# Nyström attention with two expert layers on one core: the same steps in a new hand-written order

## The chip, the cores and the metric

The kernel runs on one core of a Trainium2 chip. The metric is the time of one execution in device microseconds (us). The core's engines are TensorE (PE, with its weight loads shown apart as PEld), VectorE (DVE), ScalarE (ACT), GpSimd (POOL) and SyncE (SP); each works through an instruction queue of its own in order, and they wait for one another by semaphores. Transfers between the chip's memory (HBM) and the on-chip memory (SBUF) run on 16 DMA engines and are issued by SP (stores at the end also by ACT). Products of PE land in PSUM.

## The reference

```python
def _attn_ref(q, k, v):                      # [4, 8, 576, 64], m = 32 landmarks
    q_lm = q.reshape(B, H, m, S // m, D).mean(axis=3)
    k_lm = k.reshape(B, H, m, S // m, D).mean(axis=3)
    A, Bm, C = sm(q, k_lm), sm(q_lm, k_lm), sm(q_lm, k)      # softmaxes
    Z = Bm.transpose(0, 1, 3, 2) / (norm1(Bm) * norminf(Bm) + 1e-06)
    for _ in range(6):
        Z = 2 * Z - Z @ Bm @ Z
    return A @ Z @ C @ v

def _moe_ref(x, w_in, w_out):                # 2304 tokens, 512 -> 2048 -> 512
    h = x @ w_in
    return (h * np.tanh(softplus(h))) @ w_out

def _moe2_ref(x, w_in, w_out):
    g = np.maximum(x @ w_in, 0.0) ** 2
    return g @ w_out
```

The output of the attention, with its heads side by side, is the input x of the first layer, and the first layer's output that of the second.

## The kernel before

The kernel is one straight program without loops on the chip. Its order is written out by hand: the string `PROGRAM` holds 2638 steps of the form `thing.step@tag+n`, and the last lines of the function call them one after the other under a manual schedule, so that each engine's queue holds its instructions in the order in which the steps issue them. `@tag` names the PSUM buffer of the step's result; `+n` puts n products of the identity with itself into that buffer ahead of the step (line 311, warm-ups). Buffers are taken from lists of free ones by tag, so a transfer's issue on SP waits until the work on the buffer's former tile is done, and the entries behind it on SP wait too.

Eight head groups, `a` to `h`, of four heads each go through the attention: `lk`, `lq`, `lv` load (L491 to L525), `tk`, `tq` turn k and q by products with the identity (L569), `tl` makes the landmark means, `pa`, `pb`, `pc` are the scores (L716, L642, L657), `pe` turns the exponentials (L682; `ET` copies them out of PSUM on ACT), `pv` multiplies them with v (L697). The groups form three batches `B0`, `B1`, `B2`; the last, the third head group of the title's change, holds four of them, `e` to `h` (their tiles end in 20, 21, 30, 31: pe31 and pv31 are those of `h`). A batch runs the six Newton steps: `n` is the product (L848, tiles nw20 to nw25 of B2), `r` copies one half of it on ACT (L861), `z` adds the other half on DVE (L865), and the next `n` needs both; `pw` (L883) and `wz` then put Z into the weights, and the folds `F` (L912) multiply these into layer 1's w_in. So each Newton step is short work on PE followed by a way over ACT and DVE, and other steps stand between two of them to keep PE at work.

Layer 1 works on pieces of tokens: `p.f` makes the hidden products (`hc`), `t.y` the products with w_out (`y`), both with three fp32r products for one fp32 product (`prod`, L930 to L932); `U` units load a weight block of 512 KB (`d`, L364 or L375), split it into a high and a low part on ACT, DVE and POOL (`lo`, `st`, `ab`, `cl`, `ad`, `hi`, `lw`). Layer 2 runs over combined halves of its matrices (a scheme with seven products for eight blocks): `W`, `X`, `Y`, `Q` and `Z` are its parts; `Q..a` and `Q..b` load weights that the kernel itself stored in HBM (L1272, L1298), `Q..p` are products with w_in (L1283 to L1285), `Q..d` sums of them on DVE (L1313), `Q..y` products with w_out into tiles O20, O21, O22 (L1356 to L1358), `Z.e` the last sums on DVE (L1250), `Z.o` the stores of the output (L1257).

Of the kernel before, what the change touches and what calls it, by code (L numbers as in the profile page):

```python
# [10 lines left out]
F32 = mybir.dt.float32  # L11
F32R = mybir.dt.float32r
U32 = mybir.dt.uint32
# [41 lines left out]
    U3.lo c.zk@y B0.n0@at B0.r0 B0.z0 U4.cl B0.n1@y+3 b.mi b.ae B0.r1 U3.st U3.ab c.xq c.zq c.TL B0.z1 B0.n2@at B0.r2
    U4.ad e.lk b.su U3.cl U3.ad d.lk B0.z2 b.pe@h b.mu B0.n3@y+2 d.sk U4.hi U4.lw c.pc@h b.ET b.lv c.pb@at c.PB b.pv@y
    B0.r3 B0.z3 B0.n4@y B0.r4 b.tb c.pa@at+1 b.ah B0.z4 B0.n5@y U0.ad d.tk@h c.cm B0.z5 b.cv d.Sk B0.pw@y U8.d U8.lo
    c.at e.lq d.Tk B0.wz d.tl@y d.TL c.ce c.am c.mi e.tk@h+1 e.Tk e.sq d.pc@at d.cm b.al d.pb@y d.PB B1.bx U5.d U5.lo
    c.pe@h U5.st f.lk U6.d@gh c.ET B1.be F00.fo@h c.ae d.ce B1.bs B1.nr@y+7 U8.st B1.rs d.pe@at f.lq B1.n0@y F00.mh
    f.tk@h U5.ab d.lv U5.cl e.Sq U5.ad U7.ab U8.ab d.ET B1.z0 B1.r0 F00.ml B1.n1@y d.pa@at B1.z1 U6.lo U6.st B1.r1  # L60
    B1.n2@y f.Tk U6.ab U7.cl U7.ad p0.f0 U5.hi c.cr B1.z2 d.at c.lv p0.f1 p0.f2 B1.r2 U6.cl p0.M0 B1.n3@y B1.r3 d.cr
    d.am U6.ad U6.hi e.lv U6.lw p0.f3 p0.M1 f.sq e.tq@h U7.hi U7.lw e.Tq B1.z3 d.pv@y d.cv f.tq@at c.pv@y e.sk p0.c0
    p0.g0 f.Tq B1.n4@y B1.r4 p1.f0 e.Sk p0.c1 B1.z4 c.su p1.f1 p1.M0 p1.c0 p1.f2 B1.n5@at B1.z5 U5.lw p1.g0 e.tl@y
    p0.g1 e.TL p1.f3 c.cv B1.pw@y B1.wz e.pc@h U8.cl U8.ad d.mi p1.M1 p1.c1 p1.g1 e.pb@at e.PB f.sk e.cm c.mu U9.d
# [1394 lines left out]
```

## Time and profile before

| | before |
|---|---|
| median of the runs | 785.86 us (785.80 to 786.46) |
| profiled execution | 784.31 us |
| its span, first to last instruction | 782.2 us |
| PE busy | 763.4 us, 5952 matmuls |
| DVE busy | 613.6 us |
| POOL, ACT busy | 387.0 us, 376.1 us |
| DMA moved | 156.73 MB, mean 200 GB/s |
| mean granted clock of PE | 0.994 |

PE is busy for 98% of the span; the 18.8 us without PE work and the stretches at a lower granted clock are what an order of the same steps can change. A fp32 product of plain operands shows as two matmuls in the trace (a Newton step of 16 products as 32), a fp32r product as one. Times in the timeline are starts and lengths from the span's start; "issue" as a releaser means that the engine waited for nothing that the profile shows. Matmul lengths overlap in the pipeline, so the text takes differences of starts.

### The profile page before, as it was taken

Reading aid. Unit: us, or ns where it says so; the run is one execution under the profiler, and the core shown is the slowest. Engines: PE = TensorE matmul, PEld = TensorE weight load, DVE = VectorE, ACT = ScalarE, POOL = GpSimd, SP = SyncE. Lnnn points to the kernel's source line nnn. Section 1 sums busy time; section 2 is a strip of 40 time slices with the busy share of each in tenths; the row PEclk is TensorE's granted clock in tenths of the full one; section 3 lists DMA queues with packets and bytes.
Section 4 is the critical chain, followed back from the end, with each engine's and each line's share of the span. In section 5 each row is a group of like instructions: output and inputs, shape, how many; then the busy total and the mean of one; then the engine's idle time right before and its main releaser. Section 6 shows DMA issues by size and latency. Waiting matters only on the chain.

```text
span 782.2 us, 15515 instructions
## 1 busy us (share of the span) xinstructions
PE 763.4 (98%) x5952; PEld 713.0 (91%) x5952; DVE 613.6 (78%) x964; ACT 376.1 (48%) x622; POOL 387.0 (49%) x265
## 2 busy tenths in 40 slices
PE   6999999899999999999999999999999999999997
PEld 5778989698999999999999988999999999999996
DVE  7899877488686877779789889866786888776785
ACT  6798887454674564646553333342333331332240
POOL 2544332242333543525466877786464585635440
PEclk9999999899999999999999999999999999999999
DMA  9672462201231455666729898898988797668853
GB/s 323 214 223 85 132 187 82 83 28 55 82 108 54 149 188 176 228 203 230 243 94 300 246 297 251 282 307 293 301 268 277 224 307 250 225 223 271 276 171 81
DMA packets 87721, 156.73 MB, mean 200 GB/s; under 512 B 9184, under 2 KB 37088, under 8 KB 87648
## 3 DMA queue, kind: packets, MB, share of 16 engines
q1 hardware_dynamic: 86976, 154.96, 61.1%
q10 hardware_dynamic: 672, 0.79, 0.4%
q8 instruction: 47, 0.77, 0.4%
q14 instruction: 26, 0.21, 0.1%
HBM read 119.54 MB, written 36.18 MB: 199 GB/s over the span
## 4 chain that ended last, share of the span: by engine, by line
PE 93%; DMA 3%; DVE 2%; ACT 1%; issue 1%; SPq 0%; POOL 0%; ACTq 0%; DVEq 0%; POOLq 0%
PE y L930 9%; PE y L931 8%; PE y L932 8%; PE P L1283 7%; PE P L1285 7%; PE P L1284 7%; PE hc L930 5%; PE hc L931 4%; PE hc L932 4%; PE O L932 4%; PE O L931 4%; PE O L930 4%; PE O L1358 3%; PE O L1357 3%; PE O L1356 3%; PE m L912 2%
## 5 line engine op out<-in xcount | busy, mean ns | idle before, releaser
L1177 POOL TENSOR_TENSOR ringglx<-A,ringghx 128x768 fp32r<-128x768 f32 x40 | 76.7, 1936 | 63.9 <-ACT ringghx L1172 63.9
L1172 ACT CAST ringghx<-A 128x768 fp32r<-128x768 f32 x40 | 33.0, 836 | 78.8 <-DVE A L1149 27.5
L1313 DVE TENSOR_TENSOR U<-U,P 128x384 f32<-128x384 f32 x72 | 39.8, 552 | 36.4 <-PE P L1285 35.0
L932 PE MATMUL O<-b,ringglx 128*128 128x256 f32 x240 | 67.8, 282 | 0.0
L931 PE MATMUL O<-b,ringghx 128*128 128x256 f32 x240 | 67.8, 282 | 0.0
L981 DVE TENSOR_TENSOR ringglx<-sc,ringghx 128x576 fp32r<-128x576 f32 (+2 forms) x80 | 63.5, 820 | 5.3 <-ACT ringghx L976 5.3
L930 PE MATMUL O<-b,ringghx 128*128 128x256 f32 x240 | 67.7, 282 | 0.0
L1015 DVE TENSOR_TENSOR acc<-acc,y 128x384 f32<-128x384 f32 x72 | 39.3, 549 | 30.9 <-PE y L932 30.7
L963 ACT ACTIVATE sc<-hc 128x576 f32<-128x576 f32 x64 | 41.4, 654 | 40.6 <-PE hc L932 28.0
L976 ACT CAST ringghx<-sc 128x576 fp32r<-128x576 f32 (+2 forms) x80 | 44.1, 576 | 18.2 <-PE y L932 17.4
L932 PEld LDWEIGHTS O<-b,ringglx 128*128 128x128 f32 x240 | 45.8, 191 | 0.0
L931 PEld LDWEIGHTS O<-b,ringghx 128*128 128x128 f32 x240 | 45.7, 191 | 0.0
L930 PEld LDWEIGHTS O<-b,ringghx 128*128 128x128 f32 x240 | 45.7, 190 | 0.0
L1313 DVE TENSOR_TENSOR A<-U,P 128x384 f32<-128x384 f32 x56 | 30.1, 549 | 19.3 <-PE P L1285 15.9
L410 POOL TENSOR_TENSOR wa<-rawwi 128x512 int32<-128x512 int32 x16 | 19.0, 1191 | 42.8 <-DVE rawwi L397 39.3
L1293 ACT COPY U<-P 128x384 f32<-128x384 f32 x24 | 11.5, 481 | 57.8 <-PE P L1285 47.5
L403 POOL TENSOR_TENSOR wi<-rawwi 128x512 int32<-128x512 int32 x16 | 19.3, 1213 | 39.2 <-DVE rawwi L397 33.4
L417 POOL TENSOR_TENSOR rawwo<-rawwo 128x512 int32<-128x512 int32 x14 | 15.9, 1135 | 41.9 <-DVE rawwo L397 17.0
L1154 DVE TENSOR_TENSOR A<-A,A 128x768 f32<-128x768 f32 x28 | 34.8, 1244 | 1.1
L1203 DVE TENSOR_TENSOR sum<-sum,O 128x768 f32<-128x768 f32 x32 | 29.9, 948 | 6.1 <-PE O L932 6.1
L1149 DVE SCALAR_TENSOR_TENSOR A<-A 128x768 f32<-128x768 f32 x28 | 33.1, 1198 | 0.4
L383 DVE SCALAR_TENSOR_TENSOR rawwo<-rawwo 128x512 uint32<-128x512 uint32 x30 | 28.1, 935 | 6.1 <-ACT rawwo L380 6.1
(1377 smaller groups left out, 2857.7 us busy)
## 6 DMA issues: line engine op xcount, KB each, us to landing
b<-sc SPq DMA_DIRECT2D x98, 256.0 KB, 4.1
rawwo<-in_moe_w_out_dram SPq DMA_DIRECT2D x30, 512.0 KB, 4.6
rawwi<-in_moe_w_in_dram SPq DMA_DIRECT2D x24, 512.0 KB, 4.3
rawwi<-in_moe_w_in_dram SPq DMA_DIRECT2D x16, 256.0 KB, 3.0
st<-wh SPq DMA_DIRECT2D x8, 512.0 KB, 3.9
st<-ws SPq DMA_DIRECT2D x8, 512.0 KB, 3.8
sc<-sd SPq DMA_DIRECT2D x16, 256.0 KB, 3.9
out_dram<-o SPq DMA_DIRECT2D x58, 64.0 KB, 2.7
```

What stands on the lines that cost most here:

```text
L930: nc.tensor.matmul(ps, wh, rh, start=start, stop=False)
L931: nc.tensor.matmul(ps, wh, rl, start=False, stop=False)
L932: nc.tensor.matmul(ps, wl, rh, start=False, stop=stop)
L963: nc.scalar.activation(s, self.hs[hf][:, :, :CH], AF.Mish)
L976: nc.scalar.copy(self.at_ring("gh", hf, c0, e - a), self.s[hf][:, :, a:e])
L981: nc.vector.tensor_tensor(lo, self.s[hf][:, :, a:e], hi.bitcast(F32), ALU.subtract)
L1015: nc.vector.tensor_tensor(a, a, ps, ALU.add)
L1177: nc.gpsimd.tensor_tensor(lo, self.A[self.src(k)], hi.bitcast(F32), ALU.subtract)
L1283: nc.tensor.matmul(ps[:, :TT], wh[:, c], xh[:, c, :], start=c == 0, stop=False)
L1284: nc.tensor.matmul(ps[:, :TT], wh[:, c], xl[:, c, :], start=False, stop=False)
L1285: nc.tensor.matmul(ps[:, :TT], wl[:, c], xh[:, c, :], start=False, stop=c == 1)
L1313: nc.vector.tensor_tensor(to, x, self.ps[i][:, :TT], ALU.add)
```

## The change

`PROGRAM` holds the same 2638 steps in another order, from its first line to its last; 20 warm-up suffixes are put elsewhere, in all 19 warm-up products for 20. No function changes. Since the string grew by one line, every line number behind it is higher by one. Three pieces of the difference, the Newton steps of B2 and the program's end:

```diff
-    p7.M0 B2.n0@at B2.r0 B2.z0 h.pa@h+1 B2.n1@y B2.r1 B2.z1 g.pe@at g.ET h.pe@h B2.n2@y h.ET B2.r2 t4.e0 h.at B2.z2
...
-    Q27.y0 Q26.y3 Q27.y3 Z2.e0 Z2.o2 Z2.e3 Q26.y1 Q27.y1 Z2.e1 Z2.o0 Z2.o3 Z2.o1
...
+    B2.z2 h.ET t4.y0 g.lv t4.e0 g.pv@y g.cv B2.n3@y B2.z3 B2.r3 h.pv@y h.mi h.ae g.su B2.n4@at B2.z4 p7.f2 p7.f3 f.su
...
+    Q07.o1 Q27.y2 Z2.e5 Z2.e4 Q07.o2 Q26.y0 Z1.o2 Z2.o5 Z2.e3 Q27.y0 Z2.e2 Z2.e0 Z2.o4 Z2.o3 Q26.y1 Z2.o2 Z2.o0 Q27.y1
```

In the rows below a name is a tile and its number; x16 is the count of like products in a row.

PE's queue around the Newton steps nw22 to nw25 of B2, before (`hc` belongs to a `p.f` step of layer 1):

```order
L848 MATMUL nw22__2108<-inv2_1978 32x64 x16
L697 MATMUL pv30_2135<-three3x3_75,ET30_2099 32x64 x2
...
L848 MATMUL nw23__2163<-inv2_1978 32x64 x16
L697 MATMUL pv31_2183<-three3x3_75,ET31_2125 32x64 x24
L848 MATMUL nw24__2211<-inv2_1978 32x64 x16
L930 MATMUL hc7_1_2229<-three1x9_1227,mh11_1547 128x288
...
L932 MATMUL hc7_1_2229<-three1x9_1227,ml11_1548 128x288
L848 MATMUL nw25__2243<-inv2_1978 32x64 x16
```

The same place now:

```order
L849 MATMUL nw22__2092<-three3x3_75 32x64 x16
L931 MATMUL y0110_2118<-ringghx7_1010,wo0_4h_1600 128x384
...
L933 MATMUL y0110_2118<-ringghx7_1010,wo0_7l_1825 128x384
L698 MATMUL pv30_2134<-three3x3_75,ET30_2112 32x64 x2
...
L849 MATMUL nw23__2160<-three3x3_75 32x64 x16
L698 MATMUL pv31_2179<-v310_1107,three3x3_75 32x64 x2
...
L849 MATMUL nw24__2210<-three3x3_75 32x64 x16
L931 MATMUL hc7_1_2228<-three1x9_1243,mh11_1561 128x288
...
L933 MATMUL hc7_1_2228<-three1x9_1243,ml11_1562 128x288
L849 MATMUL nw25__2247<-three3x3_75 32x64 x16
```

Twelve `y` products have come between nw22 and pv30, twelve `hc` products stand between nw24 and nw25, and the `hc` products that followed nw25 are gone from there.

SP's queue of transfers, before, from the load of v for group `g` (step `g.lv`) on (rawwo0_14 is unit U30, rawwi0_11 U19, rawwi0_12 U24, rawwo0_15 U31, rawwo0_9 U21, rawwi0_13 U25):

```order
L525 DMA three3x3_75<-in_v_dram 96x2x384
L525 DMA three2x2_74<-in_v_dram 96x2x384
L364 DMA rawwo0_14_1839<-in_moe_w_out_dram 128x1024
L375 DMA rawwi0_11_1924<-in_moe_w_in_dram 128x1024
L375 DMA rawwi0_12_2209<-in_moe_w_in_dram 128x1024
L364 DMA rawwo0_15_2273<-in_moe_w_out_dram 128x1024
L364 DMA rawwo0_9_2341<-in_moe_w_out_dram 128x1024
L375 DMA rawwi0_13_2458<-in_moe_w_in_dram 128x1024
```

The same stretch now:

```order
L365 DMA rawwo0_7_1723<-in_moe_w_out_dram 128x1024
L376 DMA rawwi0_11_1922<-in_moe_w_in_dram 128x1024
L365 DMA rawwo0_14_1967<-in_moe_w_out_dram 128x1024
L376 DMA rawwi0_13_2056<-in_moe_w_in_dram 128x1024
L526 DMA three3x3_75<-in_v_dram 96x2x384
L526 DMA three2x2_74<-in_v_dram 96x2x384
L365 DMA rawwo0_9_2339<-in_moe_w_out_dram 128x1024
L376 DMA rawwi0_9_2540<-in_moe_w_in_dram 128x1024
L365 DMA rawwo0_15_2584<-in_moe_w_out_dram 128x1024
```

U30 and U25 stand ahead of the load of v, U21 directly behind it, and U31 comes behind U17 (rawwi0_9).

PE's queue at the end of the program, before, the first product of each group of six (q26w and q27w tell Q26 from Q27; the O20 groups are first y0, then y1; O21 and O2last are y3):

```order
L1356 MATMUL O20_8952<-q27w7_8829,three0x12_4432 128x512
...
L1356 MATMUL O21_8932<-q26w7_7497,three1x13_4818 128x256
...
L1356 MATMUL O2last_8965<-q26w7_7497,three1x13_4818 128x256
...
L1356 MATMUL O21_8932<-q27w7_8829,three0x12_4432 128x256
...
L1356 MATMUL O2last_8965<-q27w7_8829,three0x12_4432 128x256
...
L1356 MATMUL O20_8952<-q26w7_7497,three1x13_4818 128x512
...
L1356 MATMUL O20_8952<-q27w7_8829,three0x12_4432 128x512
```

The same now:

```order
L1357 MATMUL O21_8868<-q27w7_8143,three0x12_4507 128x512
...
L1357 MATMUL O20_8963<-q26w7_8665,three1x13_4817 128x512
...
L1357 MATMUL O20_8963<-q27w7_8143,three0x12_4507 128x512
...
L1357 MATMUL O20_8963<-q26w7_8665,three1x13_4817 128x512
...
L1357 MATMUL O20_8963<-q27w7_8143,three0x12_4507 128x512
```

The products of y3 have gone ahead of y0, and y1 follows y0 directly.

At the program's start the loads stand in the order q of `a`, k of `a`, U2, q of `d`, U1, k of `b`, q of `b`; before it was k of `a`, q of `a`, q of `d`, U2, k of `b`, U1, q of `b`. In layer 2 the `a` and `b` steps of `Q` and the stores by `sv` and `h` steps stand at other places among the same products.

## Rows read from the trace of the kernel before

**Rows 1.** the page's busy times: engine, us, share of the span, instructions.

```profile
PE 763.4 (98%) x5952; PEld 713.0 (91%) x5952; DVE 613.6 (78%) x964; ACT 376.1 (48%) x622; POOL 387.0 (49%) x265
```

**Rows 2.** PE's waits: waited-for, us in total, times, longest.

```profile
PE pv L697 <- issue: 3.4, 1, 3.4
```

**Rows 3.** PE's timeline, 133 to 153: start, us, form and count, [idle before].

```profile
133.45 0.44 PE L930 MATMUL y<-ringghx,wo_4h 128*128 128x384 f32 x1
...
135.64 0.30 PE L930 MATMUL hc<-three1x,mh 128*128 128x288 f32 x1
...
136.53 0.65 PE L848 MATMUL nw__2044<-inv 32*32 32x64 f32 x32
...
141.74 0.65 PE L848 MATMUL nw__2163<-inv 32*32 32x64 f32 x32
...
142.32 0.75 PE L697 MATMUL pv<-three3x,ET 96*32 96x64 f32 x37
...
146.49 0.64 PE L697 MATMUL pv<-three3x,ET 96*32 96x64 f32 x11 [3.42 <-issue]
...
147.06 1.08 PE L848 MATMUL nw__2211<-inv 32*32 32x64 f32 x32
...
148.07 0.61 PE L930 MATMUL hc<-three1x,mh 128*128 128x288 f32 x1
...
149.81 1.08 PE L848 MATMUL nw__2243<-inv 32*32 32x64 f32 x32
...
150.81 0.61 PE L930 MATMUL hc<-three1x,mh 128*128 128x288 f32 x1
...
152.28 0.34 PE L930 MATMUL y<-ringghx,wo_4h 128*128 128x384 f32 x1
```

**Rows 4.** DMA queues: whole run; 134.4:143.9; 140:143; 143.9:144.1; 148.0:149.2 (packets, MB, share).

```profile
q8 instruction: 47, 0.77, 0.4%
...
q1 hardware_dynamic: 411, 1.54, 47.6%
...
DMA packets 296, 1.10 MB, mean 366 GB/s; under 512 B 28, under 2 KB 28, under 8 KB 296
...
q8 instruction: 1, 0.02, 29.3%
...
q8 instruction: 1, 0.02, 4.6%
```

**Rows 5.** SP's timeline, 128 to 166: its queue's transfers, start and us.

```profile
138.38 0.80 SPq L364 DMA_DIRECT2D rawwo<-in_moe_w_out_dram  x2
...
139.23 0.43 SPq L375 DMA_DIRECT2D rawwi<-in_moe_w_in_dram  x1
```

**Rows 6.** windows: length, busy us and count of PE, PEld, DVE, ACT, POOL; clock, DMA.

```profile
146.40:152.00 5.60, 5.51 (x86) 4.72 (x86) 3.02 (x7) 0.27 (x1) 2.19 (x2) 0.50 0.01 3
...
396.00:470.00 74.00, 71.58 (x376) 66.03 (x375) 63.84 (x91) 27.32 (x46) 51.36 (x40) 1.00 0.75 239
```

**Rows 7.** the end's timeline, PE and DVE: start, us, form, [idle before].

```profile
772.30 0.28 PE L1356 MATMUL O<-q26w,three1x 128*128 128x256 f32 x1
...
772.50 0.75 DVE L1250 TENSOR_TENSOR o<-sum,O 128x256 f32<-128x256 f32 x2 [1.97 <-PE O L1358]
...
775.17 0.40 PE L1356 MATMUL O<-q26w,three1x 128*128 128x512 f32 x1
```

**Rows 8.** the start: PE and SP by time; DMA issues, 2.6 to 4.5, us to landing.

```profile
12.43 1.09 PE L569 MATMUL tk<-ident,ringglx 128*128 128x128 f32 x8
...
3.19 0.48 SPq L508 DMA_DIRECT2D ringglx<-in_k_dram  x1
...
DMA packets 178, 0.75 MB, mean 393 GB/s; under 512 B 16, under 2 KB 16, under 8 KB 178
...
ringglx<-in_k_dram SPq DMA_DIRECT2D x1, 576.0 KB, 8.0
```

**Rows 9.** chain of the work that ended last, 396 to 470: start, us, what.

```profile
457.26 4.33 DMA q04w<-st
```

More of the change, by code (lines that the diff above doesn't have):

```diff
@@ L55 @@
[L55 to L64, printed above, removed]
@@ L80 @@
-    f.mu B2.r4 B2.n5@at g.mu p7.f3 p7.M1 p7.c1 B2.z5 U31.d@T t4.y1 g.tb h.cv U31.lo B2.pw@at B2.wz e.ah t4.e1 t4.y2
-    t4.e2 h.mi f.tb F20.fo@at F30.fo@h U21.d U21.lo h.ae h.su t4.y3 F20.mh F20.ml F30.mh p7.g1 t5.y0 e.al U21.st t4.e3
-    f.ah h.mu h.tb f.al h.ah t5.e0 p8.f0 p8.f1 p8.M0 t5.y1 F30.ml U21.ab U21.cl g.ah p8.c0 t5.y2 U19.ab t5.e1 U21.ad
-    U21.hi t5.e2 U21.lw U31.st U31.ab p8.f2 U25.d@T U25.lo p8.f3 t5.y3 p8.M1 p8.c1 p8.g1 p8.g0 p9.f0 U26.d p9.f1 h.al
-    p9.f2 p9.f3 p9.M0 t5.e3 p9.c0 p9.g0 U30.cl g.al p10.f0 F21.fo@at U30.ad p9.M1 p9.c1 p10.f1 p10.f2 U19.cl U19.ad
@@ L205 @@
[L205 to L207 removed]
+    a.lq a.tq@h a.sq x.m x.e a.lk a.Tq a.tk@h a.Sq U2.d@m a.sk d.lq U2.lo U2.st a.Sk d.sq a.tl@y+1 a.Tk a.TL a.pb@y+4
+    a.pc@h a.cm U1.d@m U2.ab b.lk U2.cl U2.ad b.xk a.pa@at a.at a.am a.ce a.cr a.PB b.tk@h b.Tk U1.lo U1.st b.lq
@@ new lines @@
+    h.cr t3.e2 B2.rs t3.y3 U30.lo p7.f0 p7.f1 p6.M0 p6.c0 p6.g0 p6.c1 p6.g1 h.pa@h f.am p7.M0 B2.n0@at B2.r0 f.mi
+    h.pe@h+1 U25.d@T U25.lo B2.z0 B2.n1@y B2.r1 g.pe@at+1 f.ae t3.e3 B2.z1 h.at B2.n2@y B2.r2 h.am g.ET p7.c0 U30.st
+    B2.z2 h.ET t4.y0 g.lv t4.e0 g.pv@y g.cv B2.n3@y B2.z3 B2.r3 h.pv@y h.mi h.ae g.su B2.n4@at B2.z4 p7.f2 p7.f3 f.su
+    f.mu B2.r4 B2.n5@at B2.z5 h.su t4.y1 h.cv B2.pw@at h.mu U19.lo B2.wz p7.M1 p7.c1 t4.e1 f.tb p7.g0 t4.y2 U19.st
+    t4.e2 t4.y3 e.mu e.tb e.ah e.al U21.d h.tb p7.g1 f.ah t4.e3 F20.fo@at F30.fo@h F30.mh F30.ml F20.mh F20.ml t5.y0
@@ new lines @@
+    t5.e0 t5.y1 t5.e1 f.al p8.f0 p8.f1 p8.f2 p8.f3 g.mu U21.lo g.tb U21.st U21.ab U21.cl h.ah h.al t5.y2 p8.M0 p8.c0
+    g.ah U21.ad t5.y3 t5.e3 U21.hi p8.M1 p8.g0 p8.c1 p8.g1 U19.ab t5.e2 p9.f0 p9.f1 p9.M0 p9.f2 p9.c0 p9.f3 g.al p9.M1
+    p10.f0 U21.lw p9.g0 p9.c1 p9.g1 p10.f1 p10.f2 U30.ab U30.cl U30.ad U17.d p10.M0 t6.y0 t6.y1 U17.lo U17.st U17.ab
+    U19.cl U19.ad U17.cl U17.ad t6.e0 t6.e1 U31.d@T U31.lo t6.y2 U31.st U31.ab t6.e2 F21.fo@at F21.mh p10.f3 U26.d
+    F21.ml U26.lo t6.y3 p10.c0 p10.g0 p10.M1 p10.c1 p10.g1 F31.fo@at p11.f0 p11.f1 p11.M0 p11.c0 p11.g0 U25.st U26.st
@@ new lines @@
+    t7.y0 t7.e0 U26.ab p11.f2 p11.f3 U25.ab U25.cl U25.ad U24.d@T U24.lo t6.e3 U24.st U26.cl U26.ad U24.ab t7.y1 t7.y2
+    t7.e1 F31.mh F31.ml p11.M1 p11.c1 t7.y3 p12.f0 p12.f1 t7.e2 U16.d U31.cl p11.g1 t7.e3 U16.lo U16.st U16.ab U16.cl
+    U16.ad p12.M0 p12.c0 p12.g0 U24.cl t8.y0 t8.e0 t8.y1 t8.e1 U23.d U23.lo U23.st U24.ad t8.y2 t8.e2 U23.ab U23.cl
+    U23.ad p12.f2 p12.f3 p13.f0 p12.M1 p12.c1 p12.g1 t8.y3 U23.hi U23.lw U18.d U18.lo U18.st p13.f1 p13.M0 p13.c0
+    p13.g0 U34.d@T p13.f2 p13.f3 p14.f0 p13.M1 p13.c1 p13.g1 t9.y0 t8.e3 U18.ab U34.lo U18.cl U18.ad U27.d p14.f1
@@ new lines @@
+    Y13.t1 Y13.t3 Y13.h0 Y13.l0 Y13.t2 Y12.l6 Q21.a1 Y13.b1 Y13.b0 Y13.p1@h Y13.a1 Q21.a0 Q22.a6 Q21.p1 Y13.h1 Q21.p2
+    Q22.a2 Q22.a0 Q21.s Q21.d1 Q22.p1 Q22.s Q22.a3 Y20.r0 Y12.b4 Y12.p3@h Y13.h4 Y12.a3 Q21.a3 Q21.a5 Q21.p6 Q21.a6
+    Q21.a4 Q21.p7 Q21.d2 Y13.h5 Q21.d3 K7.sv1 Q21.p5 Y13.l4 Y20.b3 Y13.h3 Y13.l3 Y13.b9 Q21.p4 Q21.d4 Q21.d5 Y20.b0
+    Y13.b11 Q21.d6 Y13.p6@h Q24.a6 Y20.r2 Y13.b6 Q22.p2 Q23.a4 Q21.p3 Y12.a6 Y13.a6 Y13.p5@h Q27.a4 Q21.d7 Y20.r1
+    Y13.a5 Y13.h2 Y13.l2 Y20.r3 Y20.t1 Y20.t3 Q22.p6 Y20.h3 Y13.b12 Y13.b13 Q26.a0 Y13.l1 Y13.t4 Y13.p4@h Z1.u2 Y20.h2
@@ L208 @@
+    Q07.o1 Q27.y2 Z2.e5 Z2.e4 Q07.o2 Q26.y0 Z1.o2 Z2.o5 Z2.e3 Q27.y0 Z2.e2 Z2.e0 Z2.o4 Z2.o3 Q26.y1 Z2.o2 Z2.o0 Q27.y1
+    Z2.e1 Z2.o1
 """
```

276 lines of the change are left out of this document (135 added, 141 removed).

## The prediction

> **What bounds the kernel now.** I read the page's busy times first: TensorE (PE) is busy 763.4 us of a span of 782.2 [rows 1], so the kernel takes PE's work plus PE's idle time, 18.8 us in all. The change leaves the products as they are (one warm-up fewer), so only idle time and the speed of single products can move. Next I read what PE waited for. The largest entry behind the first load is odd: 3.42 us in which the profile shows no releaser, only "issue", in line 697 [rows 2]. The timeline around it shows more: the second `pv` of the pair (step `h.pv`, tile pv31) stops after 37 of its 48 matmuls and goes on with the other 11 only at 146.49 [rows 3]. Nothing can be waited for in the middle of such a group: its operands are those of the 37 before.
>
> I take it for a fetch of instructions. Queue 8, of kind instruction, moved 47 packets of 16 KB [rows 4]; PE has 5952 matmuls and as many weight loads [rows 1], 11,904 instructions, so one packet is about 253 of them, in fact 256. Counted in the trace from the first instruction, the break stands after the 3777th; the block that ran out had been begun 256 instructions earlier, in nw22 at about 140.5, and I take that as the moment at which the next one was asked for. From 134.4 to 143.9 no instruction packet arrived: all 411 packets are of queue 1 [rows 4]. That queue was full because SP had just issued three weight transfers of 512 KB, two at 138.38 and one at 139.23 [rows 5], 296 packets of them between 140 and 143 [rows 4]. The packet came at 143.98, took 0.94 us (29.3% of 16 engines for 0.2 us) [rows 4], and PE resumed 1.57 us behind its end. The next one shows the fetch without company: PE resumes at 146.49 [rows 3], its packet comes at 148.09 and takes 0.88 us (4.6% of 16 engines for 1.2 us) [rows 4]. So a fetch on quiet DMA engines takes 1.60 + 0.94 + 1.57 = 4.1 us, with others 140.5 to 146.49, 6.0 us.
>
> The pause costs twice. From 146.40 to 152.00 the granted clock is 0.50 [rows 6], the lower of the two levels, after 3.4 us without work. I price it by pairs of starts in [rows 3]. Newton products (`nw`): 147.06 to 148.07 is 1.01 and 149.81 to 150.81 is 1.00, against 0.58 from 141.74 to 142.32; 0.85 lost. Six `hc` products: 1.74 and 1.47, against 0.89 from 135.64 to 136.53; 1.43 lost. The 11 matmuls: 0.57 against 11 x 0.75 / 37 = 0.22; 0.35 lost. Together 2.6; at full clock some 0.1 would return as waiting between two Newton steps. I take 2.5.
>
> **The change part by part.**
>
> The Newton chain of the third head group. In the new order twelve `y` products stand between nw22 and pv30, and nothing of the kind stands there now. Counted in the new order, blocks again begin at the 3521st and 3777th instruction: the first is now inside those twelve products, the second again inside pv31, at about its 40th matmul. The time from one to the other has two ends. If the fetch is asked for when the block is executed, seven `y` products remain; twelve take 2.19 (133.45 to 135.64), so 1.3, then pv30 0.97 (48 x 0.75 / 37), nw23 0.58, and 40 of pv31 0.81: 3.7 us. If the sequencer runs ahead of the array and asks as soon as nw22 is let go, 0.58 + 2.19 + 0.97 + 0.58 + 0.81 = 5.1 us. The quiet fetch needs 4.1. What is left of the stall is 0 to 0.4 us plus what the estimate of 1.57 can be off; I take 0.4, nearer to the first end. Such a pause is an eighth of the present one, so I count no fall of the clock.
>
> It rests on quiet DMA engines. On SP the three transfers are U31, U21 and U25 now, U31 being let go by `h.pa`. In the new order U25 and U30 stand ahead of the chain, U21 waits for a unit that POOL finishes ahead of the chain, and U31 stands behind U17, which waits for U21's unpacking, well behind the chain. The only other transfers of that stretch, two of `v` for pv30, wait for nothing on SP and go out ahead of the chain too. So the stall loses 3.42 - 0.4, and the 2.5 of the clock go: -5.5.
>
> [...]
>
> The end. Now the last pair of `y` products into O20 (step Q26.y1) stands behind the y3 pair: DVE's two sums of e0 start at 772.50 and take 0.75 while PE works from 772.30 to 775.17, and y1 starts without a wait [rows 7]. In the new order Q26.y1 stands directly behind Q27.y0. Both write the same PSUM tile, so PE waits until DVE has read y0's result. No row shows that wait; its size is the 0.20 from PE's next start to DVE's (772.30 to 772.50), the 0.75, and a handover back of some hundredths: +1.0. Below 0.75 it cannot be, since DVE cannot begin before y0's last product; above, DVE has e2 in front of e0, so 0.75 to 1.4 with half of e2's two sums in the way. The tail behind the last product keeps its two sums and its stores.
>
> The start. The second part of k (`b.lk`) is issued at 3.19, lands 8.0 later at 11.2, and is wanted by PE at 12.43 [rows 8]: 1.2 us spare. It moves behind the 512 KB of U1; at 393 GB/s [rows 8] that is 1.3 later, so a wait of 0.1, and 1.3 if PE comes there earlier by all of the spare. The second part of q keeps its place but is wanted about one group of transposes sooner. I take +0.5, with 0 and 1.3 for ends. One warm-up fewer is 0.2 at most; left out.
>
> Layer 2's transfers. From 396 to 470 PE idles 74.00 - 71.58 = 2.4 us [rows 6], on late weights and on late sums. The new order puts the weight loads (`a` and `b` steps of Q) and SP's stores at other places nearly everywhere, and no row says how they meet. One end is that all 2.4 go; the other that one transfer is issued when wanted, as in the chain, where q04w counts 4.33 from issue to landing [rows 9]. I take -0.4, near nothing, as 71.58 of those 74 us are busy already.
>
> The sum, on the profiled execution: 784.31 - 5.5 + 1.0 + 0.5 - 0.4 = 779.9. The runs' median, 785.86, is 1.55 above that execution's time, so 781.4. From no change a measurement of this kernel tells about 0.2%, 1.6 us.
>
> **The rivals.**
>
> A weight transfer of layer 2 comes late (slower than before). SP issues in order; if one entry waits for room in front of a Q weight, this lands 4.33 behind its issue with PE at its first product. The price is 4.3 of idle time and, as PE's clock fell after 3.4 us here, 2.5 of half clock: 6.8, so 788.2. It decides when the issue comes less than 4.3 us ahead of its use. For it: SP's queue is full there, and q04w was late already. Against: it was late by little, and the order moves many of these loads forward as well.
>
> The stall stays where it is. [...] Then the start and the end alone count: 785.86 + 1.0 + 0.5 - 0.4 = 787.0, within 0.2%. For it: the block again ends inside pv31. Against: the stop in mid-group, the queue-1 packets, and one packet of queue 8 just before PE resumes.
>
> All goes. No stall, no start wait, and all of layer 2's 2.4: 785.86 - 3.42 - 2.5 - 2.4 + 1.0 = 778.5. For it: a sequencer that runs ahead. Against: the start's spare is small.
>
> **How the numbers follow.** Forecast 0.67, a late weight 0.12, the stall stays 0.12, all goes 0.09. Of the forecast 0.03 ends within 0.2%, the late weight is slower in 0.11, and the stall that stays is the same in 0.10 and slower in 0.02. So faster 0.64 + 0.09 = 0.73, same 0.03 + 0.01 + 0.10 = 0.14, slower 0.13. The forecast's own range: below, 779.0 with layer 2 better by 2.4; above, 784 with the start at 1.3, the end at 1.4 and a full microsecond of stall. The range reaches on to the stall that stays, 787.0, and leaves out the late weight and half of the case below.
>
> **What would show it.** Right: pv31 in one piece or with a pause under 1 us, clock 1.00 from 140 to 160, no transfer of 512 KB issued in the 5 us before pv31; a wait of PE of some 1.0 on DVE's line 1250 (1251 in the new numbering) 3 us before the last product; a wait of tenths at `b.tk`. Wrong: a pause of 3 us at pv31 with quiet DMA engines; a low clock elsewhere; a wait of several us on a `q..w` weight.

## The result: 776.4 us, a gain twice that of the forecast

The changed kernel takes 776.44 us (776.26 to 776.69), the kernel before 785.83 in the same comparison: a ratio of 0.988, 95% interval 0.9862 to 0.9897. Forecast were 781.4, with 779.0 as the lower end of the forecast's own range. The direction was right, the size was not: 9.4 us instead of 4.5. (Over the 75 runs of before in the five later comparisons the median is 785.2, so the gain on record here is some 0.6 us on the high side.)

The page's busy times of the changed kernel, to be held against [rows 1]:

```profile
PE 760.0 (98%) x5950; PEld 710.5 (92%) x5950; DVE 596.4 (77%) x964; ACT 375.1 (48%) x621; POOL 379.8 (49%) x265
```

Its span is 774.5 us, so PE idles 14.5 us instead of 18.8, and its work shrank by 3.4 us though all products are the same but for one warm-up; some 2.4 of it is the clock in the Newton chain, as the windows below and b_hold show. PE's waits (what was waited for, us in total, times, longest), in place of [rows 2]:

```profile
PE tq L570 <- DMA ringghx<-in_q_dram: 4.8, 1, 4.8
...
PE O L1357 <- DVE o L1251: 0.8, 1, 0.8
...
PE P L1284 <- DVE U L1314: 0.6, 1, 0.6
```

The 3.42 us of "issue" in pv are gone. The Newton chain, PE's timeline (start, length, form), against [rows 3]:

```profile
138.25 0.65 PE L849 MATMUL nw__2092<-three3x 32*32 32x64 f32 x32
...
138.83 0.44 PE L931 MATMUL y<-ringghx,wo_4h 128*128 128x384 f32 x1
...
141.92 0.65 PE L849 MATMUL nw__2160<-three3x 32*32 32x64 f32 x32
...
143.33 0.65 PE L849 MATMUL nw__2210<-three3x 32*32 32x64 f32 x32
...
143.91 0.40 PE L931 MATMUL hc<-three1x,mh 128*128 128x288 f32 x1
...
145.70 0.48 PE L849 MATMUL nw__2247<-three3x 32*32 32x64 f32 x20
```

pv31 stands whole between nw23 at 141.92 and nw24 at 143.33: 1.41 us with nw23's 0.58, so 0.83 for its 48 matmuls. Every Newton step takes 0.58 again. Windows (length, busy us and count of PE, PEld, DVE, ACT, POOL, then clock, DMA share, GB/s) of the same 30 us and of the stretch of layer 2 in [rows 6]:

```profile
130.00:160.00 30.00, 30.00 (x512) 25.84 (x512) 21.84 (x49) 16.43 (x28) 11.59 (x9) 1.00 0.01 2
...
400.00:470.00 70.00, 69.64 (x360) 63.83 (x359) 59.02 (x90) 28.36 (x47) 49.73 (x41) 1.00 0.86 275
```

PE does not idle from 130 to 160 at all and has the upper clock level, 1.00; in layer 2 the 2.4 idle us have become 0.36 (0.36 from 396 on, too). SP's transfers around the chain, against [rows 5], and the instruction packet that the chain lives on, against [rows 4] (0.2 us from 139.3, with its share of 16 engines):

```profile
122.65 0.35 SPq L365 DMA_DIRECT2D rawwo<-in_moe_w_out_dram  x1
...
166.98 0.35 SPq L376 DMA_DIRECT2D rawwi<-in_moe_w_in_dram  x1
...
q8 instruction: 1, 0.02, 41.2%
```

Between 122.65 and 166.98 SP issued nothing, and the packet came at 139.4, some 3.8 us before PE reached the end of the block (near 143.2, inside pv31).

Where the profiled executions differ, by sums over PE's records (a gap is time without any matmul):

| | before | after | difference |
|---|---|---|---|
| first matmul | 4.68 | 4.76 | +0.07 |
| matmul work | 763.40 | 759.95 | -3.45 |
| of it nw20 to pw of B2, without gaps | 14.43 | 13.62 | another order |
| gaps up to 28 us | 1.60 | 2.33 | +0.73 |
| gaps 28 to 75 us | 1.31 | 0.97 | -0.33 |
| gaps in the chain of B2 | 3.50 | 0 | -3.50 |
| gaps in layer 2 | 3.59 | 1.51 | -2.07 |
| gap at the end | 0 | 0.84 | +0.84 |
| behind the last matmul, to the span's end | 4.17 | 4.17 | 0 |
| outside the span | 2.06 | 1.82 | -0.25 |
| profiled execution | 784.31 | 776.35 | -7.96 |

Of the 3.45 us of matmul work 2.5 lie in the lines that make the chain (pv, nw, pw, folds, hc, y), 0.5 in transposes, scores and warm-ups and 0.5 in layer 2's products. The pair of profiles leaves 1.43 us of the 9.4: the median of before lies 1.52 above its profiled execution, that of the changed kernel only 0.09. Three things were therefore open: whether the pause of pv31 is what I took it for, what of layer 2 is the order's doing, and what the other executions of before lose.

### The profile page after: what moved, and what is told of

The parts are those of the page before. It is cut to its first block, busy times and chain, and to the rows that moved or that the text cites. A ratio compares the mean times of both kernels' runs of the same rounds, so it can differ in the third digit from the quotient of the medians.

```text
span 774.5 us, 15494 instructions
## 1 busy us (share of the span) xinstructions
PE 760.0 (98%) x5950; PEld 710.5 (92%) x5950; DVE 596.4 (77%) x964; ACT 375.1 (48%) x621; POOL 379.8 (49%) x265
## 4 chain that ended last, share of the span: by engine, by line
PE 92%; DVE 3%; DMA 3%; ACT 1%; issue 1%; SPq 0%; DVEq 0%; ACTq 0%
PE y L931 9%; PE y L933 9%; PE y L932 9%; PE P L1284 7%; PE P L1285 7%; PE P L1286 7%; PE hc L931 5%; PE hc L932 4%; PE hc L933 4%; PE O L933 4%; PE O L932 4%; PE O L931 4%; PE O L1359 3%; PE O L1358 3%; PE O L1357 3%; DMA rawwi<-in_moe_w_in_dram 2%
## 5 line engine op out<-in xcount | busy, mean ns | idle before, releaser
L1178 POOL TENSOR_TENSOR ringglx<-A,ringghx 128x768 fp32r<-128x768 f32 x40 | 78.3, 1974 | 62.2 <-ACT ringghx L1173 57.2
L982 DVE TENSOR_TENSOR ringglx<-sc,ringghx 128x576 fp32r<-128x576 f32 (+2 forms) x80 | 54.8, 703 | 21.5 <-ACT ringghx L977 21.2
L1314 DVE TENSOR_TENSOR A<-U,P 128x384 f32<-128x384 f32 x56 | 30.7, 550 | 19.8 <-PE P L1286 17.6
L1204 DVE TENSOR_TENSOR sum<-sum,O 128x768 f32<-128x768 f32 x32 | 30.3, 950 | 17.7 <-PE O L933 17.6
L384 DVE SCALAR_TENSOR_TENSOR rawwi<-rawwi 128x512 uint32<-128x512 uint32 x32 | 28.1, 886 | 5.6 <-ACT rawwi L381 3.8
L1155 DVE TENSOR_TENSOR A<-A,A 128x768 f32<-128x768 f32 x28 | 29.7, 1062 | 0.9
```

The source lines that it names most:

```text
L982: nc.vector.tensor_tensor(lo, self.s[hf][:, :, a:e], hi.bitcast(F32), ALU.subtract)
L1178: nc.gpsimd.tensor_tensor(lo, self.A[self.src(k)], hi.bitcast(F32), ALU.subtract)
L1314: nc.vector.tensor_tensor(to, x, self.ps[i][:, :TT], ALU.add)
```

## The experiments

In the diffs a line is a piece of `PROGRAM`. The "order of before" and the "changed order" are the two programs compared above. A program that is joined from both takes the steps of one up to a number and then, in the order of the other, all steps that are still to be done; the diff of such a program gives this rule, not the text of `PROGRAM`.

### The pause: transfers or products

**b_hold**, the order of before with the transfers held back:

```diff
-    B2.z5 U31.d@T t4.y1 g.tb h.cv U31.lo B2.pw@at B2.wz
+    B2.z5 t4.y1 g.tb h.cv H.w U31.d@T B2.pw@at B2.wz
...
+        def w(self):
+            note = dram.tile([P, 64], F32, tag="note", name="note")
+            nc.sync.dma_start(note, batches[2].cv[:, 3, :])
```

> The order of before; only SP's three weight transfers U31, U21, U25 are held back until the last pv of the chain is copied out (a 32 KB store of that copy stands ahead of them on SP; ACT's first step on U31 and U21 moves back with them). No products are put between nw22 and pv30. Theory 1, the fetch of instructions is held up by those transfers: in the changed kernel the instruction packet starts 1.05 us after the array is 64 instructions short of the block, so here it is asked for near 139.0, comes near 140.1 and is usable before PE runs dry at 143.07; no pause, clock 1.00, 3.4 + 2.5 = 5.9 us and what the unprofiled runs lose on top, 778 to 780.5. Theory 2, the fetch needs the time that the twelve y products give, transfers or not: a pause of 1 to 3.4 us stays, 782.5 to 786. Theory 3, the pause is no fetch: it stays whole, 785.8.

Measured: 780.63 us, 5.1 under before in the same comparison (785.72). PE's timeline and the packet:

```profile
144.37 0.65 PE L848 MATMUL nw__2163<-inv 32*32 32x64 f32 x32
...
146.06 0.41 PE L697 MATMUL pv<-three3x,ET 96*32 96x64 f32 x11 [0.36 <-issue]
...
146.40 0.65 PE L848 MATMUL nw__2211<-inv 32*32 32x64 f32 x32
...
147.97 0.65 PE L848 MATMUL nw__2243<-inv 32*32 32x64 f32 x32
...
q8 instruction: 1, 0.02, 30.7%
```

The pause is still at the same place, 37 matmuls before it and 11 behind, but takes 0.36 us instead of 3.42; the Newton steps behind it have the length 0.65 that they have at full speed, so the clock did not fall (1.00 in the windows from 146 to 152). The program ahead of the chain is the one of before and the whole chain came 2.63 us later in this execution, so the packet at 143.7 would have been at 141.1 there: 2.9 earlier than the 143.98 of [rows 4], and the pause is 3.06 shorter. Theory 1 was right on what holds the packet up, and too hopeful by the 0.36. (b_holdwarm below, quiet too, has 0.89 there, so quiet DMA engines leave some tenths of pause and not a fixed one.)

**b_y**, the twelve products alone:

```diff
-    B2.z2 h.am g.pv@y
+    B2.z2 h.am t4.y1 g.pv@y
...
-    B2.z5 U31.d@T t4.y1 g.tb h.cv U31.lo B2.pw@at B2.wz e.ah t4.e1 t4.y2 t4.e2
+    B2.z5 U31.d@T g.tb h.cv U31.lo t4.e1 t4.y2 B2.pw@at B2.wz e.ah t4.e2
```

> The order of before; only twelve y products (step t4.y1) go from behind nw25 to between nw22 and pv30, and the next twelve (t4.y2) ahead of pw in their place. The transfers go out at 138.4 as before. Theory 1: the packet still comes only near 144 and is usable near 145.5 to 146.5, while PE now runs dry near 145; a pause of 0.5 to 1.5 us, too short for the clock to fall, 779 to 782. Theory 2: no pause, 778 to 780. Theory 3: the pause stays, 785.8.

Measured: 783.71 us (782.47 to 787.72, before 785.72).

```profile
147.19 0.58 PE L697 MATMUL pv<-three3x,ET 96*32 96x64 f32 x25 [0.76 <-ACT inv L861]
...
147.99 0.54 PE L697 MATMUL pv<-three3x,ET 96*32 96x64 f32 x23 [0.22 <-issue]
...
153.34 0.44 PE L930 MATMUL y<-ringghx,wo_4h 128*128 128x384 f32 x1 [1.66 <-ACT cv L705]
...
q8 instruction: 1, 0.02, 29.7%
```

The break in pv31 now stands behind 25 matmuls and not 37. Twelve matmuls earlier, with twelve products and their twelve weight loads put in ahead: a break that moves by just the instructions inserted hangs on the count of instructions, as the end of a block would, and theory 3 falls. The count says it more sharply: with PE's matmuls, weight loads and semaphore instructions counted from the start, the break stands behind the 3777th instruction in all twelve profiles here that have one, whether that is behind 25, 30, 37, 38, 40 or 41 matmuls of pv31. The packet is late, at 145.8, with the transfers in flight (DMA share 0.83 from 143 to 146); the cover of the products leaves 0.22 us of pause, less than expected. The time is above theory 1's 779 to 782: the edit pays elsewhere, as the second twelve products wait 1.66 us, and PE's clock falls there (0.76 of the upper level on the mean from 152 to 156). So its time says little; its timeline does.

**a_noy**, the changed order without the twelve products there:

```diff
-    B2.z2 h.ET t4.y0 g.lv t4.e0 g.pv@y
+    B2.z2 h.ET g.lv g.pv@y
...
-    B2.n5@at B2.z5 h.su t4.y1
+    B2.n5@at B2.z5 t4.y0 t4.e0 h.su t4.y1
```

> The changed order; only the twelve y products (t4.y0 and its sum) go from between nw22 and pv30 back to behind nw25. DMA stays quiet. Theory 1: the packet comes near 139.4, usable near 142; PE would be dry near 141.2; a pause of 0 to 0.8 us at most and no fall of the clock, 776.2 to 777.5. Theory 2: a pause of 1.5 us or more, with the fall of the clock if it is over 3: 778 to 782.

Measured: 780.27 us, 3.8 more than the changed kernel, outside what theory 1 gave, and yet without a pause for instructions (the wait for ACT, which nobody expected, gave the fetch its time, so this run does not tell what a quiet fetch leaves there):

```profile
140.56 0.25 PE L698 MATMUL pv<-three3x,ET 96*32 96x64 f32 x2 [1.57 <-ACT ET L691]
...
141.37 1.08 PE L849 MATMUL nw__2146<-three3x 32*32 32x64 f32 x32
...
143.00:146.00 3.00, 3.00 (x77) 2.66 (x67) 1.89 (x6) 1.38 (x5) 0.00 (x0) 0.69 0.02 5
```

pv30 waits 1.57 us for ACT, which copies the exponentials out of PSUM, and then the clock falls: Newton steps at 1.08, 0.69 of the upper level on the mean from 143 to 146. In the order of before the first of these copies, `g.ET`, is issued ahead of `h.pe` and nw22; in the changed order it stands behind nw22, in front of the twelve products. So the twelve products are needed in the changed order, but to cover ACT's copy; neither theory had that. nw20 to pw takes 17.48 us here and 13.62 in the changed kernel, 3.86, the whole loss.

**a_load**, the changed order with transfers in flight:

```diff
-    h.ET t4.y0 g.lv t4.e0 g.pv@y
+    h.ET t4.y0 g.lv L.w L.d0 L.d1 L.d2 t4.e0 g.pv@y
...
+        def w(self):
+            note = dram.tile([P, 32], F32, tag="note", name="note")
+            nc.sync.dma_start(note, chunks[7].s[0][:, 0, :32])
+
+        def d(self, k):
+            t = dram.tile([P, 2 * DM], U32, tag=f"dump{k}", name=f"dump{k}")
+            nc.sync.dma_start(t, w1i.bitcast(U32)[k * P : (k + 1) * P, : 2 * DM])
```

> The changed order, with its twelve y products; added on SP's queue, once ACT has done its step of chunk 7 at about 135.1, are a 16 KB store and three transfers of 512 KB from HBM to HBM, which move from some 137 to 142 and which nothing waits for. Theory 1: the packet that came at 139.39 comes at 141.5 to 143.5 and is usable 1.6 to 2.5 later, PE runs dry near 143.2: a pause of 0 to 2.5 us, 776.5 to 779, more with a fall of the clock. Theory 2 and theory 3: no pause, 776.4.

Measured: 779.43 us (779.05 to 779.86), 3.0 more than the changed kernel. PE's timeline, the queue of the transfers from 138 to 142.8 and the packet:

```profile
145.26 0.32 PE L698 MATMUL pv<-v,three3x 96*32 96x64 f32 x7 [1.77 <-issue]
...
q1 hardware_dynamic: 446, 1.64, 98.7%
...
q8 instruction: 1, 0.02, 30.0%
```

Transfers delay the packet from 139.4 to 142.8 and bring the pause back, 1.77 us in pv31 with 7 matmuls to come, twelve products ahead of it or not. Of the four, this one shows the cause most plainly: nothing changed but the traffic. There are four transfers of 512 KB and not three: the load of U21, which stands behind the added ones on SP, goes out at 137.65 instead of 122.65. The clock stayed at 1.00 here; from nw20 to pw it is 1.98 more than in the changed kernel, and of the 2.8 between the two profiles 0.2 lie ahead of the chain, 0.4 behind it and 0.2 outside the span, not explained further.

### Layer 2 and the end

**h_ba900**, the order of before for 900 steps, then the changed one:

```diff
+    order = before[:900] + [step for step in after if it is still to be done]
```

> The first 900 of the 2638 steps in the order of before, the others in the order in which the changed kernel has them: before's start and Newton chains, the changed layer 2 and end. Theory L, the new places in layer 2 are worth what the two traces show, 2.1 us of PE's waits, less 0.84 for the wait of the end: 1.2 less than before, 784.5, and PE's gaps between 395 and 730 under 1.8 us. Rival, the waits went because all of the changed kernel came earlier or otherwise: PE's gaps in layer 2 stay near 3.6, 785.7 to 786.6.

Measured: 783.54 us against 785.19, 1.65 less. PE's waits:

```profile
PE pv L697 <- issue: 2.9, 1, 2.9
...
PE O L1356 <- DVE o L1250: 0.8, 1, 0.8
...
PE P L1283 <- DVE U L1313: 0.6, 1, 0.6
...
PE P L1283 <- DVE A L1313: 0.5, 1, 0.5
...
PE P L1283 <- DVE C L1313: 0.3, 1, 0.3
```

The pause of the chain is there (2.89), and in layer 2 the three waits of the changed kernel stand in place of those of before, gaps of 1.48 us in place of 3.59. Those of before were six:

```profile
PE P L1283 <- DVE C L1313: 0.8, 1, 0.8
PE O L1357 <- POOL wo_4l L432: 0.8, 1, 0.8
PE y L931 <- DVE ringglx L981: 0.8, 1, 0.8
PE P L1283 <- DMA q04w<-st: 0.5, 1, 0.5
PE P L1283 <- DMA q14w<-st: 0.4, 1, 0.4
PE P L1283 <- DMA q00w<-st: 0.3, 1, 0.3
```

Three of them, 1.2 us, were late weights, two, 1.6, operands that POOL and DVE finished late; none of these five is left, and the waits that are left are all on DVE's sums. All nine profiles with the layer 2 of before have gaps of 2.3 to 3.7 us there, 3.2 on the mean; all nine in the changed order 1.3 to 1.7, mean 1.5. So the order of layer 2 is worth 1.7 by itself, less the 0.84 of the end. The other 0.8 of the 1.65 that the runs gained is not explained.

**a_best**, the end mended, and the second part of k ahead of U1:

```diff
-    a.cm U1.d@m U2.ab b.lk
+    a.cm b.lk U1.d@m U2.ab
...
-    Q27.b3 Q27.y4 Q27.y5 Q27.y3 Z2.u7 Z2.u8 Q07.o1 Q27.y2 Z2.e5 Z2.e4 Q07.o2 Q26.y0 Z1.o2 Z2.o5 Z2.e3 Q27.y0 Z2.e2
-    Z2.e0 Z2.o4 Z2.o3 Q26.y1 Z2.o2 Z2.o0 Q27.y1 Z2.e1 Z2.o1
+    Q27.b3 Q27.y4 Q27.y5 Z2.u7 Z2.u8 Q07.o1 Q27.y2 Z2.e5 Z2.e4 Q07.o2 Q26.y0 Z1.o2 Z2.o5 Q27.y0 Q27.y3 Z2.e0
+    Z2.o4 Z2.e3 Z2.e2 Z2.o0 Q26.y1 Z2.o3 Z2.o2 Q27.y1 Z2.e1 Z2.o1
```

> The changed order with two repairs: the y3 products of Q27 stand between y0 and y1 at the end, so that DVE's e0 runs under them, and the second part of k is issued ahead of U1. Theory: 0.84 from the end, 0.3 to 0.6 from the start: 775.0 to 775.3. Rival, the tail takes up what the end gives since more stores are left for the last microseconds: 775.8 to 776.2.

Measured: 774.80 us (774.70 to 774.94), the fastest version and a little better than forecast: 1.64 us under the changed kernel, in the profiles 0.78 from the start's waits and 0.84 from the end, ratio to before 0.9863 (0.9841 to 0.9886). PE has no gap behind 620.3 us; at the end DVE's two sums of e0 (the first two of this group) run beside products:

```profile
764.53 1.14 DVE L1251 TENSOR_TENSOR o<-sum,O 128x256 f32<-128x256 f32 x3 [2.67 <-PE O L1359]
```

The step of the forecast on the end was right in mechanism and size: in the changed kernel PE waits 0.84 us for DVE's line 1251, here not at all, and the tail grows by 0.1 (4.17 to 4.26).

**a_best2** moved one thing more:

```diff
-    b.lq b.tq@h b.Tq a.mi a.ae a.su d.tq@h+1 a.pe@at
+    b.lq d.tq@h b.tq@h b.Tq a.mi a.ae a.su a.pe@at
```

> a_best with the eight transposes d.tq put ahead of b.tq and without their warm-up: the wait for the second part of q, 0.55 in a_best, would be filled by them. 774.2 to 774.5; if another wait takes its place, 774.8.

Measured: 775.33 us, no gain: the wait went to d.tq (0.91 us, for ACT) and 0.84 came at pb.

### What the other executions of before lose

**b_look1** and **b_look2** are the kernel before, unchanged.

> The kernel before, unchanged, one more look. Theory S: full speed from 11 us or later and the products of the mark at 72 us later than 72.5. Rival S0: full speed by 9, the mark at 72.1 to 72.3, and what its time has above 784.3 lies at the pause.

> The kernel before, unchanged, a second look; the theories expect of it what they expect of b_look1.

Measured: 784.31 and 785.34 us. PE's timeline of the same eight transposes `b.tk`, in b_look2 (with the window over them, its clock the third number from the end) and in the changed kernel:

```profile
13.14 1.97 PE L569 MATMUL tk<-ident,ringglx 128*128 128x128 f32 x8
...
13.14:15.04 1.90, 1.90 (x14) 1.57 (x9) 1.74 (x4) 0.70 (x2) 0.00 (x0) 0.50 1.04 425
...
12.91 1.06 PE L570 MATMUL tk<-ident,ringglx 128*128 128x128 f32 x8 [0.62 <-DMA ringglx<-in_k_dram]
```

The same eight products take 1.9 us from start to the next start in the one and 0.9 in the other; in the profiled execution of before they took 1.0 (12.43 to 13.45, the first in [rows 8]). In b_look2 the clock column has the lower level for them, 0.50. But PE's products begin at half the rate in every profile: the first eight take 1.74 us from start to the next start in the profiled execution of before (4.68 to 6.42), where the column says 1.00; it tells only from the first change on record on. When full speed comes to stay differs. With before's start the last slow transpose or warm-up begins at 8.3 us in the profiled execution and at 8.6 in h_ba900, but at 13.8, 14.1, 14.0, 15.3 and 16.8 in b_y, b_look1, s_ba70, b_look2 and b_hold; in b_look1 and b_look2 the rate had doubled by 8 to 9 us and halved again behind the waits near 9 and 10 (0.74 and 1.13 us in b_look1). With the changed order's start (seven profiles, one of them without its warm-ups) it is 7.4 to 10.3. So the profiled execution of before was one of two in seven. nw20 starts at 136.53 in it and at 137.9 to 139.2 in the four late ones, 1.4 to 2.6 later.

The chain then gives some of it back: from nw20 to pw the profiled execution took 17.93 us, b_look1 and b_look2 16.70 and 17.05, b_hold without the long pause 12.47. The pause is about the same in the first three (3.16 to 3.45), but the clock costs 2.4 in the first and 1.4 to 1.5 in b_look1 and b_look2. Both of these start late, as theory S has it, and yet b_look1 takes the 784.31 us of the execution that started early: its nw20 is 1.4 later, its pw only 0.2. So a late start alone does not account for the 1.5 us between the median and the profiled execution.

**b_warm**, four warm-ups into the wait ahead of a.pc:

```diff
-    a.tl@y a.TL a.pc@h a.pa@at+1
+    a.tl@y a.TL a.pc@h+4 a.pa@at+1
```

> The order of before; only four warm-up products more, ahead of a.pc, where PE waits 1.0 to 1.1 us for ACT near 9.5. In the looks at before, b_hold and b_y, whose first 130 us are the same program, the products run at half speed until 8.5, 16.7 and 13.7 us, and the first pb of group b starts at 21.8, 24.4 and 23.2; with the changed order, which has four warm-ups ahead of a.pb, the step to full speed lies near 8.6 to 10 in two looks. Theory S, that this pause decides how long PE stays at half speed, so that most runs of before lose 1.4 to 2.6 us which its profiled run did not lose: 783.5 to 784.8, the runs closer together, full speed from 9 to 11. Rival, the start is left to chance whatever PE does there: 785.5 to 786.5, since the four products cost 0.2 to 0.8 more than the pause.

Measured: 783.13 us (781.94 to 785.58) against 785.19. The last slow product begins at 10.2 us, and nw20 at 136.82. But the sixteen added instructions (fifteen on balance, with one semaphore instruction fewer) also moved the block's end in pv31 (30 matmuls ahead of it, 18 behind), and nw20 to pw is 16.62 where executions with an early start have 17.6 to 18.3: the 2.1 us are not the start's alone. Hence:

**b_warm2**, the same with four fewer in a later place, so that the blocks end where they did:

```diff
-    a.TL a.pc@h a.pa@at+1
+    a.TL a.pc@h+4 a.pa@at+1
...
-    B1.nr@y+7
+    B1.nr@y+3
```

> The order of before with the same two warm-up edits; the pause at pv31 stays where it was, 37 products before it and 11 behind. Theory S: 784.0 to 784.6. Rival S0: 785.0 to 786, and b_warm's 2.1 came from the block boundary that its 16 instructions moved.

Measured: 784.57 us against 785.15 (ratio 0.9992, 0.9983 to 1.0002): no clear difference. The start is early (9.5 us, nw20 at 136.61), the break is one matmul later than meant (38 ahead of it, 10 behind), and nw20 to pw takes 18.33.

**b_holdwarm**, b_hold and b_warm2 together:

> b_hold (transfers held back, so hardly a pause at pv31) with four warm-up products more ahead of a.pc and four fewer ahead of B1.nr, so that all later blocks of instructions begin where they did. With the pause gone the runs tell of the start alone. Theory S, the pause of 1.1 us near 9.5 us leaves PE at half speed for longer in most runs of before: 778.6 to 779.8, against b_hold's 780.6, runs within 0.6 us of one another. Rival S0, the start is worth nothing on the mean: 780.3 to 781.2.

Measured: 780.18 us against b_hold's 780.63, above the range of theory S; relative to before in their own comparisons the two are alike (ratios 0.9931 and 0.9930). The start is early (8.0) and the pause is 0.89, but in this profile the clock falls at 50 us (0.77 on the mean from 50 to 56), behind the waits that the four missing warm-ups left (PE idles 1.65 us from 44 to 50, 0.89 in before; in b_warm2 1.65 too, and the clock reads 1.00 there), and nw20 comes at 137.97 after all.

**a_nowarm**, the changed order without its five warm-ups at the start:

```diff
-    a.tl@y+1 a.Tk a.TL a.pb@y+4
+    a.tl@y a.Tk a.TL a.pb@y
```

> The changed order without the five warm-up products (ten matmuls) ahead of a.tl and a.pb at the start. Theory S, they bring PE to full speed early: half speed lasts beyond 11 us, 777.5 to 779, and the runs spread over more than 1 us. Rival, the order of the loads or of the steps does it: 775.5 to 776.6, since the products themselves take 1.1 to 1.5 us that would otherwise be waits.

Measured: 777.17 us (776.56 to 777.50), 0.7 more and between the two ranges. In its one profile the start is early all the same (8.0 us) and PE waits 0.91 us in place of the warm-ups.

**s_ab140**, the changed order for 140 steps, then that of before:

```diff
+    order = after[:140] + [step for step in before if it is still to be done]
```

> The first 140 steps in the order of the changed kernel (its loads, its warm-ups and the first head groups), the others in the order of before: the pause at pv31, layer 2 and the end stay as they were. Theory S: the changed start spares what before's runs lose there, 2.1 as in b_warm and a few tenths of waits behind it: 782.8 to 783.6. Rival, the start gives nothing by itself: 785 to 786.

Measured: 786.03 us against 785.10, so no gain but a loss of 0.1% (ratio 1.0011, 1.0002 to 1.0020), as the rival has it. The start is early (9.6), nw20 at 137.47 after 0.8 us more of waits than in before's profiled execution; the pause is 3.62 and nw20 to pw 18.09.

**s_ba70**, the other way round:

```diff
+    order = before[:70] + [step for step in after if it is still to be done]
```

> The first 70 steps in the order of before (some 25 us), the others in that of the changed kernel: its Newton chains, transfers, layer 2 and end stay. Theory S: the start costs what the other looks at before's start lost: 777.6 to 779, the runs spread over more than 1 us. Rival, the start is worth nothing: 776.4.

Measured: 784.44 us; it tells nothing of the start, as the joined order makes PE wait 5.21 us at 26.7 for DVE's work on B0, with a fall of the clock (0.91 on the mean from 0 to 60), which neither kernel has.

**b_sum** joins the three edits that had worked alone:

```diff
-    a.TL a.pc@h a.pa@at+1
+    a.TL a.pc@h+4 a.pa@at+1
...
-    B2.z5 U31.d@T t4.y1 g.tb h.cv U31.lo B2.pw@at B2.wz
+    B2.z5 t4.y1 g.tb h.cv H.w U31.d@T B2.pw@at B2.wz
...
+    order = this[:901] + [step for step in after if it is still to be done]
```

> Three edits to the order of before at once: the transfers held back (as in b_hold), the four warm-ups ahead of a.pc (as in b_warm), and from step 901 on the order of the changed kernel (as in h_ba900). Alone they gave 5.1, 2.1 and 1.65 us. If the gain of the change is these three and they add up, 785.2 to 785.8 less 8.85: 776.3 to 777.0, the changed kernel's time within a microsecond, and runs close together. If one of them hides another, or the twelve y products are needed after all, 778 or more.

Measured: 777.34 us (776.90 to 777.98), within 0.9 us of the changed kernel, a little above the range. The pause is 0.27, the clock 1.00 throughout, nw20 to pw 12.39. The gains are nearly additive, and all but some 0.9 of the 9.4 us is in these three. Which part of it the four warm-ups bring is not shown: b_hold and h_ba900 make 6.7 of the 8.4 against before in this comparison, and alone, without a moved block, the warm-ups gave 0.6 at most.

## Why the prediction was wrong in size

The median came 5.0 us under the forecast. In the forecast's own terms 1.7 of it is layer 2, 1.5 the offset between profiled execution and median, 0.95 matmul work outside the chain, for which there was no term, and 0.5 the pause; the start took 0.3 back, and the end, the gaps from 28 to 75 us and the time outside the span make up the rest. So two steps failed above all, the size of the layer 2 term and the offset.

- **The pause, right.** It was a fetch of instructions held up by the three weight transfers: a_load brings it back by traffic alone, b_hold takes it away by quiet alone, and the break moves with the instructions inserted. Forecast -3.0, measured -3.42 (-3.50 with the other gap of the chain). The 0.4 that I kept is of the size that b_hold (0.36), b_sum (0.27) and b_holdwarm (0.89) show; it is not there in the changed kernel, where the packet was asked for before the block ahead of it was executed: it started at 139.39, while PE was in the third of the twelve products, and the 3521st instruction (3777 less the 256 of a packet, last section) ran at 139.63. My first end for the request, at execution, does not hold there.
- **The twelve products, right by accident.** They were to give the fetch its time. In the order of before it does nearly as well without them when DMA is quiet (b_hold), and with them the pause comes back when DMA is not (a_load); in the changed order they cover ACT's copy (a_noy), which I had not seen.
- **The clock, right.** Forecast -2.5. Against b_hold's 12.03 without gaps, the profiled execution of before spent 14.43 from nw20 to pw: 2.4.
- **The end, right.** Forecast +1.0, measured +0.84 and gone again in a_best.
- **The start, half wrong.** The waits grew by 0.73 (forecast +0.5), 0.62 of it at `b.tk` as said; that half speed lasts for different times in different executions of before I did not see, and I left the warm-ups aside as "0.2 at most".
- **Layer 2, the term mis-sized.** Forecast -0.4, "near nothing, as 71.58 of those 74 us are busy already"; measured -2.07 in the pair of profiles, and h_ba900 shows that the order of layer 2 does it by itself, by taking away the late weights and the waits for POOL and DVE. A small share of idle time says nothing on how much of it an order can take away. The end of my own bound, -2.4, was nearly reached. (The lower end of the range, 779.0, counts the 0.4 twice: with all of the 2.4 it would be 779.4.)
- **The work outside the chain, a missing term.** The products outside the chain took 0.95 us less, half of it in transposes, scores and warm-ups, half in layer 2. No run takes this apart.
- **The offset, a step that failed.** "The runs' median, 785.86, is 1.55 above that execution's time" was added to the sum as if it belonged to both kernels. It belonged to before: the changed kernel's executions lie within 0.43 us, their median 0.09 above the profiled one, while those of before range from 782.7 to 787.9 over all comparisons, with medians of 785.10 to 785.75 in the five later ones. What lifts them is not shown. The start's half speed and the loss of clock at the pause both differ from one execution to the next, by 1 to 2.6 us each, but in b_look1 they nearly cancel; without the long pause and its fall of the clock the runs spread less (1.6 us in b_hold, 1.1 in b_sum).
- **The rivals.** "All goes", 778.5 with a chance of 0.09, was the nearest, and still 2 us short, 1.5 of it by the offset. The late weight did not happen: no wait of PE in layer 2 is on a transfer any more. Nor did "the stall stays", 787.0 with a chance of 0.12: of the 47 packets in before only one made PE wait, the one that met three transfers, by 3.42 us, and of the 47 in the changed kernel none, as PE has no wait on "issue" there.

Not settled: what in the changed order makes its start early in seven profiles of seven. The four warm-ups bring half speed to an end by 10.2 us in four profiles of four at before's start, but a_nowarm's one profile is early without them; and in medians an early start is worth between nothing that is clear of noise (b_warm2 0.6, b_holdwarm 0.45 under b_hold but not relative to before) and 2.1 (b_warm, with a moved block). At the long pause an early start loses again part of what it won.

## What to carry to other kernels

Where the profile says that an engine waited for "issue" in the middle of a group of like instructions, count its instructions from the start (here matmuls, weight loads and semaphore instructions): if the break stays at one count when work is inserted ahead of it, see what DMA traffic was in flight, and move the traffic first (3.42 us of pause became 0.36 in b_hold); work put ahead of the break covers the fetch too, but only as far as it goes (0.22 us of pause in b_y, 1.77 in a_load). An offset between one profiled execution and the median belongs to something: profile the kernel again before adding it to a forecast. And in a chain of short products, put work between a step and the product that needs another engine's copy, since a wait of 1.6 us there cost 3.9 with the fall of the clock behind it (a_noy).
